# Alibi sliding attention with a token mixer: half loads for batch 0, units of 64 keys in the last two batches, the mask on VectorE, and an order that counts TensorE's instructions

## The chip, the core and the metric

The kernel runs on one core of a Trainium2 chip. The core has a matrix engine (TensorE, PE in the profile; its weight loads are listed apart as PEld), VectorE (DVE), ScalarE (ACT), GpSimd (POOL), SyncE (SP), and sixteen DMA engines that move data between the chip's memory and the core's. Matmul results land in PSUM, from which only ACT and DVE copy here. The metric is the time of one execution in microseconds on the device. Lower is better.

## The reference

Eight batches, eight heads, 576 positions, 64 values per head. Attention looks back over a window of 128 positions and adds a slope per head times the distance:

```python
slopes = 2.0 ** (-8.0 * (np.arange(H) + 1) / H)
bias = slopes[:, None, None] * (-np.abs(rel))[None, :, :]
mask = (rel >= 0) & (rel < window)                    # window = 128
scores = np.where(mask, scale * q @ k^T + bias, -1e9)
attn = softmax(scores)
x = attn @ v                                          # all heads side by side: 576 x 512
```

Then a mixer over the tokens, with 64 hidden columns:

```python
W_tok = 1/8 * (x @ w_q) @ (x @ w_k)^T                 # 576 x 576
out = np.maximum(W_tok @ x, 0.0) @ w_out              # 576 x 512, fp32
```

The kernel never forms W_tok: it computes G = (x w_k)^T x, which is 64 x 512, and then G^T (x w_q)^T.

## The kernel before

**Work of one batch.** The 576 positions are four blocks of 128 and a tail of 64; tails of two neighbouring batches share tiles. The names below are those of the planner's operations.

- Loads (L): q, k and v come as fp32 and are stored as fp16 by POOL's transfers (`dma_nat`, `dma_v`, `dma_tail`, `dma_vtail`, lines 504 to 523), one per block, rows of 64 values. Four batches' worth of q, k and v tiles exist (`NNAT`, `NV`). Batch 0's first two blocks of q and k are the exception: SP loads them as fp32 (`lf`, line 549) and a cast (C) makes them fp16.
- TQ and TT turn q and k by transposes on PE (64 rows a piece, line 347); ETQ and ETT copy the result from PSUM to `qkT`, on ACT or DVE.
- A unit (`add_unit`, line 654) is one key block of 128 and one half of the heads: QK (score matmuls against 256 query columns), EXP (ACT, 128 x 1024, into a `pt` tile), MUL (DVE, times `bias`, which holds exp of slope times distance and zeros outside the window). There are eight units in a batch and ten `pt` tiles.
- PV (`add_pv`, line 694) multiplies `pt` with v, which carries a column of ones for the row sums; X divides by the sums (DVE, lines 729 and 730).
- XT/EXT turn x; WQ, WK, G and MX are the mixer's matmuls with their copies EWQ, EWK, EG; RM is the relu (ACT or DVE); OUT (512-column matmuls with `wout`) and EO give the output tile; DO stores it.

**Constants.** POOL makes an identity (`make_identity`), an iota, and two `affine_select` passes that set positions outside the window to 1e9 (`mk_mask`, line 427); DVE copies the iota to fp32 in between; ACT makes `bias` with eight exponentials (`mk_bias`, line 469).

**What sets the order.** A list scheduler (`Order.solve`, line 234) places all operations: each has allowed engines with an occupancy and a latency, dependencies, PSUM banks, and a due time (`WANT`, a table of several hundred numbers). It takes the engine that can start first, and among what can start within `WINDOW` the lowest due time. Its result is the order in which instructions are emitted; every engine then runs its own list strictly in that order, and waits on semaphores. Until the planned time 45 us, idle PE gaps are filled with matmuls on zeros (`fill`). Stores of batches 1 to 5 (`LATE`) are issued by POOL after all its loads (line 962); the others go by SP.

## Time and profile before

| | |
|---|---|
| median of 3 runs | 140.56 us (140.37 to 140.99) |
| the profiled execution's own time | 141.34 us |
| its span (first to last instruction) | 139.5 us |
| mean granted TensorE clock | 0.997 |
| PE / DVE / ACT / POOL busy | 129.3 / 112.6 / 115.2 / 110.0 us |
| instruction queue | 18 packets, 0.29 MB |
| POOL's q, k and v loads, median from issue to landing | 5.9 to 6.1 us |

The profile is of one execution. Its page gives busy time by engine, the span cut in 40 slices with the busy share in tenths, the DMA queues, the chain of waits that ended last, and groups of instructions with count and mean duration. The trace behind it answers further: busy time in chosen windows, the instructions of one engine in order of time, who waited for whom. "busy" for PE is pipelined: a matmul's own duration includes its way through the array, so neighbours overlap, and start-to-start distances tell the cost of one in a row.

### The profile page before, as it was taken

What the parts mean: (1) busy time and instruction counts of PE and PEld (TensorE: products, weight loads), DVE (VectorE), ACT (ScalarE), POOL (GpSimd) and SP (SyncE); (2) the same over time, 40 slices, a digit from 0 to 9 for tenths busy, and PEclk for the clock granted to TensorE, in tenths of its full rate; (3) what the DMA queues carried; (4) which work ended last, traced back from release to release, by engine and by line L of the source; (5) the groups of instructions that cost most, each with busy time, mean ns of one, the idle gap of its engine ahead of it and who ended that gap; (6) DMA issues with size and microseconds to landing.
All of it is one profiled execution on the core that took longest, in us unless ns stands there. A gap on an engine that the chain in (4) does not pass through costs nothing.

```text
span 139.5 us, 5462 instructions
## 1 busy us (share of the span) xinstructions
PE 129.3 (93%) x2344; PEld 81.2 (58%) x2344; DVE 112.6 (81%) x250; ACT 115.2 (83%) x175; POOL 110.0 (79%) x145
## 2 busy tenths in 40 slices
PE   6999859998999999988999999999999999999980
PEld 2345447554676367766757567765666666865530
DVE  6648997659987899989999998899999989984400
ACT  6176988399669999999999989999999999676660
POOL 7899988899995899999999999999977745600000
PEclk9999999999999999999999999999999999999998
DMA  4999999999999999999999999999999993730494
GB/s 98 184 180 154 158 153 168 152 146 154 188 215 206 158 159 153 156 155 155 154 156 153 157 156 155 159 153 156 156 215 413 358 327 144 260 153 5 167 320 189
DMA packets 117127, 25.12 MB, mean 180 GB/s; under 512 B 113072, under 2 KB 114096, under 8 KB 117104
## 3 DMA queue, kind: packets, MB, share of 16 engines
q0 software_dynamic: 110912, 20.32, 169.0%
q1 hardware_dynamic: 6192, 4.46, 10.8%
q8 instruction: 18, 0.29, 0.8%
q14 instruction: 5, 0.04, 0.1%
HBM read 29.62 MB, written 9.44 MB: 280 GB/s over the span
## 4 chain that ended last, share of the span: by engine, by line
PE 60%; DVE 16%; POOL 8%; ACT 6%; DMA 5%; issue 2%; ACTq 0%; POOLq 0%; DVEq 0%
PE pair L344 52%; PE pair L347 8%; DVE pt L687 6%; DMA nat<-in_q_dram 5%; POOL nat L506 4%; ACT pt L680 4%; DVE x L730 3%; POOL vt L521 1%; POOL natt L513 1%; DVE inv L729 1%; DVE xtl L730 1%; DVE wqT L353 1%; DVE qkT L359 1%; DVE rm L843 1%; ACT xT L357 1%
## 5 line engine op out<-in xcount | busy, mean ns | idle before, releaser
L680 ACT ACTIVATE pt<-pair 128x1024 f16<-128x1024 f32 x64 | 62.2, 1034 | 2.3 <-PE pair L344 1.7
L687 DVE TENSOR_TENSOR pt<-pt,bias 128x1024 f16<-128x1024 f16 x48 | 32.0, 684 | 2.5 <-ACT pt L680 2.3
L344 PE MATMUL pair<-wout_sb,rm 128*128 128x512 f16 (+1 forms) x132 | 31.7, 373 | 0.2
L521 POOL DMA_DIRECT2D vt<-in_v_dram x32 | 30.1, 995 | 1.6 <-DMA natt<-in_q_dram 0.8
L506 POOL DMA_DIRECT2D nat<-in_k_dram x30 | 29.1, 997 | 0.5 <-DMA nat<-in_k_dram 0.3
L506 POOL DMA_DIRECT2D nat<-in_q_dram x30 | 29.0, 987 | 0.4 <-DMA natt<-in_k_dram 0.4
L344 PEld LDWEIGHTS <-pt 128*128 128x128 f16 x576 | 20.5, 97 | 6.2 <-issue 2.6
L344 PE MATMUL pair<-vt,pt 128*128 128x65 f16 x512 | 22.9, 193 | 0.4 <-ACT pt L680 0.4
L730 DVE TENSOR_TENSOR x<-pair,inv 128x512 f16<-128x512 f32 x32 | 22.1, 692 | 1.1
L344 PE MATMUL pair<-qkT 64*128 64x256 f16 (+2 forms) x320 | 22.1, 250 | 0.6 <-ACT pt L680 0.3
L351 ACT COPY osb<-pair 128x512 f32<-128x512 f32 x29 | 17.0, 596 | 5.7 <-PE pair L344 5.5
L344 PEld LDWEIGHTS <-rm 128*128 128x128 f16 x132 | 11.3, 97 | 11.8 <-issue 1.7
L357 ACT COPY qkT<-pair 128x1024 f32<-128x1024 f32 (+1 forms) x12 | 11.4, 949 | 7.7 <-PE pair L347 7.7
L344 PE MATMUL pair<-fill 128*128 128x512 f16 x52 | 15.4, 430 | 1.8 <-DVE fill L487 1.2
L918 POOL DMA_DIRECT2D out_dram<-osb x20 | 11.2, 574 | 6.6 <-ACT osb L351 3.6
L344 PEld LDWEIGHTS <-qkT 64*128 64x128 f16 x320 | 11.1, 94 | 8.0 <-issue 5.2
L347 PE MATMUL pair<-identh,nat 64*128 64x64 f16 x512 | 10.7, 190 | 1.3 <-DMA nat<-in_q_dram 0.9
L347 PEld LDWEIGHTS <-nat 64*128 64x128 f16 x512 | 9.2, 95 | 4.0 <-DMA nat<-in_q_dram 1.3
L687 DVE TENSOR_TENSOR pt<-pt,biasl 128x1024 f16<-128x1024 f16 x16 | 10.8, 683 | 0.0
L344 PE MATMUL pair<-xT,wqq_sb 128*128 128x320 f16 (+1 forms) x64 | 10.5, 286 | 0.3 <-DVE xT L359 0.3
L357 ACT COPY xT<-pair 128x512 f32<-128x512 f32 (+1 forms) x14 | 7.4, 527 | 3.6 <-PE pair L347 2.9
L359 DVE COPY qkT<-pair 128x512 f16<-128x512 f16 (+2 forms) x14 | 9.3, 686 | 1.3 <-PE pair L347 1.1
(63 smaller groups left out, 165.5 us busy)
## 6 DMA issues: line engine op xcount, KB each, us to landing
out_dram<-osb POOLq DMA_DIRECT2D x20, 256.0 KB, 4.6
vt<-in_v_dram POOLq DMA_DIRECT2D x32, 128.0 KB, 5.9
nat<-in_k_dram POOLq DMA_DIRECT2D x30, 128.0 KB, 6.0
nat<-in_q_dram POOLq DMA_DIRECT2D x30, 128.0 KB, 6.1
out_dram<-osb SPq DMA_DIRECT2D x11, 256.0 KB, 2.3
out_dram<-osb POOLq DMA_DIRECT2D x6, 128.0 KB, 4.2
natf<-in_q_dram SPq DMA_DIRECT2D x2, 256.0 KB, 4.7
natf<-in_k_dram SPq DMA_DIRECT2D x2, 256.0 KB, 5.4
```

What stands on the lines that cost most here:

```text
L344: hold(nc.tensor.matmul(*a, **k))
L347: hold(nc.tensor.transpose(*a))
L351: hold(nc.scalar.copy(out_ap, in_ap))
L353: hold(nc.vector.tensor_copy(out=out_ap, in_=in_ap))
L357: hold(nc.scalar.copy(out_ap.bitcast(FP32), in_ap.bitcast(FP32)))
L359: hold(nc.vector.tensor_copy(out=out_ap, in_=in_ap))
L506: return lambda: nc.gpsimd.dma_start(out=nat_s[b % NNAT][j][n], in_=src[b, :, P * n:P * n + P, :].transpose([1, 0, 2]))
L521: return lambda: nc.gpsimd.dma_start(out=vt_s[b % NV][t][:, :, 0:D], in_=v[b, :, P * t:P * t + P, :].transpose([1, 0, 2]))
L680: nc.scalar.activation(out=pt[:, 0:1024], in_=two(s.bank).rearrange("p e c -> p (e c)"), func=AF.Exp, scale=SCALE)
L687: ENG2[o.eng].tensor_tensor(out=pt[:, 0:1024], in0=pt[:, 0:1024], in1=bt, op=ALU.mult)
L730: nc.vector.tensor_tensor(out=x[r].rearrange("p (g h d) -> p g h d", g=2, h=4), in0=pxv[r, :, :, 0:64], in1=inv[r].unsqueeze(3).broadcast_ ...
L918: q.dma_start(out=out[b, P * st:P * st + P, c], in_=osb)
```

## The change

Four things are changed.

1. **Batch 0's first blocks by 4 heads.** `lf` loads one half of the heads at a time on SP: eight transfers of 128 x 256 values instead of four of 128 x 512, the first halves of both blocks ahead of the second halves. Each half has its own cast, its own turn (`add_tqh`) and its own copy to `qkT`, so that a unit of one half of the heads waits for that half only.
2. **The mask on VectorE.** POOL makes only the iota. DVE makes the identity from it (`is_equal`) and the distances with the window's bounds (`mk_wdist`, `mk_dist`), one set for 128-key units and one for 64-key units.
3. **Units of 64 keys in batches 6 and 7** (`NARROW = (3,)`, the pair number). A unit is then 64 keys and all eight heads: keys sit in partitions 0 to 63 for four heads and 64 to 127 for the other four, against 192 query columns. EXP and MUL take 768 columns instead of 1024. PV takes 64 keys at a time, two row halves in turn. v has a layout of its own for it, with two halves of the partitions for two groups of heads and all nine 64-key blocks, which four transfers of 64 partitions fill; the ones columns of those tiles are set again before, and the gaps in ten `pt` tiles are cleared. The other batches keep their units, renamed `add_wunit` and `wpv`; `pt` is now a flat list of ten tiles.
4. **The planner counts TensorE's instructions.** Every PE operation says how many instructions it has (`count`); `solve` adds a delay when 256 of them would be used up in less than `FETCH` us. `STRIDE` goes from 15.2 to 13.2 and the table of due times is a new one, so the order on all engines is new.

```diff
-NPT = 5
+NPT = 10
+W = 192
+NARROW = (3,)
-STRIDE = 15.2
+STRIDE = 13.2
+FETCH = 4.8
+CHUNK = 256
+AHEAD = 191
 WANT = {
...
+            if eng == "PE" and op.count:
+                gap, wait = at - free["PE"], 0.0
...
+                while sent > mark:
+                    came = max(at, came + (FETCH if came < 104.0 else FETCH - 1.0) if mark > AHEAD else 0.0)
+                    mark += CHUNK
+                    wait = max(wait, came - at)
+                if sent + op.count > mark:
+                    then = at + wait + occ * (mark - sent) / op.count
+                    least = came + (FETCH if came < 104.0 else FETCH - 1.0) if mark > AHEAD else 0.0
+                    wait += max(0.0, least - then)
+                    came = max(then, least)
+                    mark += CHUNK
+                sent += op.count
+                end, occ = end + wait, occ + wait
...
-    def mk_ident(o):
-        make_identity(nc, ident32)
-    def mk_mask(o):
-        nc.gpsimd.affine_select(out=wm, in_=wm, compare_op=ALU.is_ge, fill=1.0e9, base=0,
-                                pattern=[[1, 256]], channel_multiplier=-1)
-        nc.gpsimd.affine_select(out=wm, in_=wm, compare_op=ALU.is_ge, fill=1.0e9, base=127,
-                                pattern=[[-1, 256]], channel_multiplier=1)
+    def mk_idh(o):
+        nc.vector.tensor_scalar(out=identh, in0=wint[:, 0:P], scalar1=0.0, scalar2=1.0,
+                                op0=ALU.is_equal, op1=ALU.mult)
+    def mk_dist(o):
+        for x in range(2):
+            r = slice(64 * x, 64 * x + 64)
+            nc.vector.tensor_copy(out=wm[r], in_=wint[r, 64 * x:64 * x + W])
+        nc.vector.tensor_scalar(out=wlo, in0=wm, scalar1=-1.0e9, scalar2=0.0, op0=ALU.mult, op1=ALU.add)
+        nc.vector.tensor_scalar(out=whi, in0=wm, scalar1=-127.5, scalar2=1.0e9, op0=ALU.add, op1=ALU.mult)
+        nc.vector.tensor_tensor(out=wm, in0=wm, in1=wlo, op=ALU.max)
+        nc.vector.tensor_tensor(out=wm, in0=wm, in1=whi, op=ALU.max)
+        nc.vector.tensor_scalar(out=wm[64:128], in0=wm[64:128], scalar1=1.0 / 16.0, scalar2=0.0,
+                                op0=ALU.mult, op1=ALU.add)
+    def mk_wdist(o):
+        nc.vector.tensor_copy(out=wwm, in_=wint)
+        for s, a in ((-1.0e9, 0.0), (1.0e9, -127.5e9)):
+            nc.vector.tensor_scalar(out=wtmp, in0=wint, scalar1=s, scalar2=a, op0=ALU.mult, op1=ALU.add)
+            nc.vector.tensor_tensor(out=wwm, in0=wwm, in1=wtmp, op=ALU.max)
...
+    def dma_v(b, t, x):
+        return lambda: nc.gpsimd.dma_start(
+            out=vn(b % NV, t)[64 * x:64 * x + 64, :, :, 0:D],
+            in_=v[b, NHP * x + 2 * t:NHP * x + 2 * t + 2, :, :].rearrange("h (n t) d -> t (h n) d", t=64))
...
+        if key not in ones or ...:
+            ones[key] = add("ones", b, "", -200 + 20 * b, DVE(0.25 if narrow else 0.5), oldv, mk_ones(b % NV, narrow))
...
-        def lf(j, n):
+        def lf(j, n, u):
+            natf = spool.tile([P, DM], FP32, name="natf", tag="late", bufs=HELD)[:, 0:256]
+            hs = slice(NHP * u, NHP * u + NHP)
+            src = (q, k)[j][0, hs, P * n:P * n + P, :].transpose([1, 0, 2])
...
+    def add_tqh(n, u, want):
+        def em(o):
+            for j in range(2):
+                for c in range(2):
+                    for h in range(2):
+                        src = nat_s[0][j][n][64 * h:64 * h + 64, 4 * u + 2 * c:4 * u + 2 * c + 2, :]
+                        flip(halves(o.bank, 4, 1)[:, h, 2 * j + c, 0, :], src.rearrange("p a b -> p (a b)"), h)
...
     def add_unit(b, g, u):
+        s = 2 * g + u
+        pt = pt_s[(8 * b + s) % NPT]
+        ptd = pt[:, 64:PTW].rearrange("p (e a c) -> p e a c", e=2, a=2)[:, :, :, 0:W]
         def em(o):
             ps = two(o.bank)
+            for a in range(2):
+                for sk, c0, n in ((s, 0, W),) if s < 7 else ((7, 0, P), (8, P, 64)):
+                    for x in range(2):
+                        for e in range(2):
+                            r = slice(64 * e, 64 * e + 64)
+                            mm(ps[64 * x:64 * x + 64, e, W * a + c0:W * a + c0 + n],
+                               t[r, 1, 2 * x + a, 64 * sk:64 * sk + 64],
+                               t[r, 0, 2 * x + a, 64 * sk:64 * sk + n], start=True, stop=True)
...
+            def rz(o):
+                nc.vector.memset(pt[:, 0:1024].rearrange("p (n c) -> p n c", c=256)[:, :, 0:64], 0.0)
...
+    def npv(b, qt):
+        sv = [sk for sk in range(2 * qt - 2, 2 * qt + 2) if 0 <= sk < 9]
+        def em(o):
+            px = two(o.bank)
+            for a in range(2):
+                for e in range(2):
+                    for i, sk in enumerate(sv):
+                        c = 64 + 256 * (2 * e + a) + 64 * (2 * qt - sk)
...
+                        for x in range(2):
+                            r = slice(64 * x, 64 * x + 64)
+                            h = 2 * a + e
+                            mm(px[:, x, 65 * h:65 * h + 65], pt_s[(8 * b + min(sk, 7)) % NPT][r, c:c + P],
+                               vn(b % NV, a)[r, e, sk, 0:65],
+                               start=(i == 0), stop=(i == len(sv) - 1))
...
-        for ns in ([0], [1], [2], [3]) if b == 0 else ([0, 1], [2, 3]):
+        if b == 0:
+            for u in range(2):
+                for n in range(2):
+                    add_tqh(n, u, base(b, 0) - 4 + n)
+        for ns in ([2], [3]) if b == 0 else ([0, 1], [2, 3]):
...
-                add_unit(b, g, u)
+                (add_unit if b // 2 in NARROW else add_wunit)(b, g, u)
```

As the program is built, PE's list has 5,094 entries instead of 4,690, DVE's 270 instead of 251, ACT's 172 instead of 169, POOL's 137 instead of 145 and SP's 24 instead of 20 (rows that differ only in being repeated are counted as one on the engines other than PE).

More of the change, by code (lines that the diff above doesn't have):

```diff
@@ L492 @@
-    zeros = add("zeros", "", "", 0, DVE(0.55), [], mk_zeros)
-    zerop = add("zerop", "", "", -59, DVE(0.45), [], mk_zerop)
-    mask = add("mask", "", "", -298, {"POOL": (0.86, 0.86)}, [dist], mk_mask)
-    mkb = [add("bias", u, "", -240 + 10 * u, ACT(1.35), [mask], mk_bias(u)) for u in range(2)]
-    sets = [add("ones", i, "", -200 + 20 * i, DVE(0.5), [], mk_ones(i)) for i in range(NV)]
-    pads = add("pads", "", "", -297, ACT(1.3), [], mk_pads)
-    mkbl = [add("biasl", u, "", 6, DVE(0.55), [mkb[u]], mk_biasl(u)) for u in range(2)]
+    idh = add("idh", "", "", -290, DVE(0.29), [iota], mk_idh)
@@ new lines @@
+    zerop = [add("zerop", i, "", -59, DVE(0.55 if 0 in NARROW else 0.3), [], mk_zerop(i)) for i in range(2)]
+    if NARROW:
+        dist = add("dist", "", "", -300, DVE(1.6), [iota], mk_dist)
+        mkb = add("bias", "", "", -240, ACT(1.14), [dist], mk_bias)
+    wide = len(NARROW) < NB // 2
+    first = {}
+    for b in range(NB):
+        first.setdefault((b % NV, b // 2 in NARROW), b)
+    ones = {}
+    pads = add("pads", "", "", -297, ACT(1.3), [], mk_pads)
+    if NARROW:
+        mkbl = add("biasl", "", "", 6, DVE(0.4), [mkb], mk_biasl)
@@ L501 @@
+    if wide:
+        zeros = add("zeros", "", "", 0, DVE(0.55), [], mk_zeros)
+        wdist = add("wdist", "", "", -90, DVE(1.5), [iota], mk_wdist)
+        wmkb = [add("wbias", u, "", -70 + 10 * u, ACT(1.35), [wdist], mk_wbias(u)) for u in range(2)]
+        wmkbl = [add("wbiasl", u, "", 6, DVE(0.55), [wmkb[u]], mk_wbiasl(u)) for u in range(2)]
     nat, natt, vt = {}, {}, {}
@@ L536 @@
     late, issues = [], []
-    loads = {}
+    loads, one_b = {}, {}
     def add_loads(b):
@@ L695, in ptc, with wpv @@
+    def wpv(b, qt):
         def ptc(kb, h, cur):
```

250 lines of the change are left out of this document (160 added, 90 removed), and 289 rows, old and new, of the table WANT.

## The prediction

> **What bounds the kernel now.** I read the page first, then the windows by stage, the chain of waits, and the timelines of single engines. The page's busy line and three of its 40-slice rows (3.49 us a slice):
>
> ```profile
> PE 129.3 (93%) x2344; PEld 81.2 (58%) x2344; DVE 112.6 (81%) x250; ACT 115.2 (83%) x175; POOL 110.0 (79%) x145
> ...
> DVE  6648997659987899989999998899999989984400
> ACT  6176988399669999999999989999999999676660
> POOL 7899988899995899999999999999977745600000
> ```
>
> No engine is the bound throughout. ACT and DVE have holes before about 42 us, are full until about 118 us, and empty again. POOL, which only issues transfers, is full until 105. The windows (columns: length, then busy time of PE, PEld, DVE, ACT, POOL with instruction counts):
>
> ```profile
> 20.00:28.00 8.00, 8.00 (x190) 5.33 (x187) 5.79 (x13) 4.49 (x6) 6.67 (x10) 1.00 1.75 158
> ...
> 60.00:85.00 25.00, 23.91 (x512) 16.06 (x509) 23.43 (x45) 24.10 (x37) 25.00 (x31) 1.00 2.42 155
> ...
> 106.00:118.00 12.00, 11.66 (x240) 7.44 (x239) 11.49 (x21) 11.79 (x20) 7.29 (x14) 1.00 0.80 301
> 118.00:124.00 6.00, 6.00 (x141) 4.78 (x141) 5.59 (x13) 3.67 (x7) 3.02 (x6) 1.00 0.74 265
> ```
>
> In the middle DVE, ACT and POOL are all above 93%; from 118 on only PE is full. The chain of waits:
>
> ```profile
> 12.94 6.91 DMA nat<-in_q_dram
> 19.84 0.05 issue
> 19.89 0.64 PE pair L347 x32
> ...
> 124.73 10.94 PE pair L344 x88
> ```
>
> It starts on batch 1's q and k, which land at 19.84, and ends on PE's output matmuls. Three timelines fix the stages: ACT's exponentials, POOL's last loads, PE's turn of batch 7's first blocks.
>
> ```profile
> 12.44 7.44 ACT L680 ACTIVATE pt<-pair 128x1024 f16<-128x1024 f32 x8 [0.78 <-PE pair L344]
> ...
> 117.52 1.96 ACT L680 ACTIVATE pt<-pair 128x1024 f16<-128x1024 f32 x2
> ```
>
> ```profile
> 98.95 1.09 POOL L506 DMA_DIRECT2D nat<-in_q_dram  x1
> 99.81 1.10 POOL L521 DMA_DIRECT2D vt<-in_v_dram  x1
> ```
>
> ```profile
> 106.01 0.64 PE L347 MATMUL pair<-identh,nat 64*128 64x64 f16 x32
> ```
>
> A load lands 6.0 us after its issue (page, transfers), so batch 7's last q or k lands at 98.95 + 5.95 = 104.9 and is turned 1.1 us later. The loads run only just ahead of the work.
>
> So there are four stages: start (to 20), a middle where ACT, DVE and loads are nearly equal, ACT's finish (106 to 119.5, the last exponential), PE's finish.
>
> **The change, part by part.**
>
> *q and k by 4 heads.* Four SP transfers of 256 KB become eight of 128 KB, first halves of both blocks first. Now the four casts start at 4.5, 4.9, 8.2 and 10.3 us (DVE timeline), and the first exponential at 12.44. In the new order of ACT's instructions the first exponential stands behind the cast that needs the seventh of the eight halves; between the third quarter (8.2) and the fourth (10.2) that is about 9.2, and with cast and queue 10.0. Ends: 8.2 (six halves suffice) and 12.4 (nothing). I take 10.0: ACT starts 2.4 us earlier, and its eight exponentials (7.44) end at 17.5 instead of 19.9. The cost is four more SP issues (0.44 to 0.9 us, SP waits for nothing then) and four more small casts, about 0.3 us each; ACT takes some of them, before its first exponential.
>
> *What is late next.* Batch 1's first turn needs the 12th POOL load before and the 15th after, since batch 0's last v blocks go ahead of it. The 15th issue of before is at 15.54 and lands 6.5 later, at 22.0. So ACT, done at 17.5, waits; batch 1 begins up to 2.2 us later, batch 0's v work and the small weights (loads 16 and 17, before 20 and 21) earlier. Between 20 and 28 ACT is busy 4.49 of 8 us, so there is a hole into which batch 0's second half can move.
>
> *Mask on DVE.* POOL loses the identity (0.49 us) and two mask instructions (0.80) with the gaps around them (about 0.7): its issues run up to 2 us earlier from the fifth on. DVE gains eleven instructions like the 128x256 cast (0.27): 3 us, and ACT four exponentials for the second bias (0.25 each, scaled from 0.31). DVE is idle for 2.3 us before 8.23; without that cover the first multiplication, now at 13.50, would wait up to 3 us, still before batch 1's load.
> Does an earlier issue land earlier? The row says little: POOL has a gap of 0.52 before its mask at 6.03, yet loads go on landing 0.85 apart, behind a queue of 6 us. From 25.5 to 40 us issues and landings both come 0.87 apart. I take 0.3 us earlier for the whole stream; ends 0 and 1.8.
> [...]
>
> *Units of 64 keys, batches 6 and 7.* An exponential falls from 1024 to 768 columns: with 1.03 us for 1024 and 0.40 for 256 that is 0.82, back to back 0.71 instead of 0.92: 16 x 0.21 = 3.4 us off ACT, half in each batch. A multiplication falls from 0.68 to about 0.54 (ends 0.51 in proportion, 0.95 if four short rows ran at the rate of the fp32 copies, 0.69 for 512): 16 x 0.14 = 2.2 off DVE. DVE gets ten clears at about 0.15 (rows: 0.085 for 32 words, 0.27 for 256) and four of 0.07: 1.8 back. PE: per batch 72 score matmuls instead of 40 and 136 PV matmuls instead of 72. Two 64-row operations run side by side in the trace: 32 turns take 0.64 us and 16 PV matmuls of 128 rows 0.66; less the last one's own 0.19 that is 15 ns and 31 ns each. At 16 the PV costs 2.2 us instead of 2.1 a batch; at 30, 4.1. Score matmuls of 192 columns go by fours, estimate 22 ns (end 40, by pairs): 1.6 against 1.9. I take the side-by-side prices: PE even. POOL issues 109 loads instead of 110, but the eight v loads of batches 6 and 7 carry 18 rows a partition instead of 16, which evens that out.
>
> *The wait that it adds.* Batch 7's v tiles are cleared anew on DVE once all of batch 3's PV is read, and the v load behind that clear is POOL's 78th, now issued at 72.1; everything behind it in POOL's queue, 31 loads, waits too. Batch 3's last PV now ends at 71.7 and its eviction would put the clear near 72.7. With the work 2 us ahead it is at 71. So POOL may stand still for up to 1 us. Loads that meet no queue land 4.7 us after issue (27 to 38 us) against 6.0 here, so 1.3 us is covered; if the work were not ahead, it would cost the stream up to 0.7. I take 0.
>
> *The order.* The count is used only in planning. It moves batch 7's second turn ahead of its first, and the first now needs the last load but one (q, block 1).
>
> **The sum,** in the span of the profiled execution (139.5; its time is 141.34, so 1.84 lies around it; median of the runs 140.56).
> - Last turn of batch 7: the load but one lands at 98.95 + 5.95 - 0.3 = 104.6; the turn's eviction on ACT starts at about 105.4 instead of 106.7: -1.3. The 2.4 us lead of the start and the lighter exponentials of batch 6 (-1.7) would bring ACT there by about 104, so the load decides, and PE, in order, waits with it.
> - From there to batch 7's last score unit ACT has eight exponentials (5.7), three relus, two output copies, two xT, one wkn and the eviction (0.92): 10.4 us; before it was 12.5 by the same prices and took 12.8. PE's own work on that stretch is 11 us (turns 0.5, outputs 4.4, scores 1.6, PV6 1.8, the rest 2.7), so PE is late next: the last unit comes at 116.2 instead of 118.0, -0.5 beyond the 1.3.
> - From the last unit to the last output PE had 16.6 us of work in 17.7; after, 16.3: -0.3, and I add 0.2 for denser code. The tail of 3.85 (copy, store, end) stays.
> Together -1.9: span 137.6, and 140.56 - 1.9 = 138.66, say 138.6 us.
>
> **Rivals.**
> *Delivery of TensorE's instructions decides: slower.* 4,688 instructions came in 18 packets of the instruction queue, 260 each. The densest long windows are 190 + 187 in 8 us and 141 + 141 in 6: 47 a us. In the new order 588 instructions stand between batch 7's second turn and batch 6's last PV, about 8.5 us of work (69 a us), and 256 around PV7 in 3.3 us. Were 47 the most, the first would take 12.5 (+4.0), the second 5.4 (+2.1). Together +6.1 against the gain of 1.9; below about 59 a us the change is slower by over 0.7: +0.7 to +4.2, 141.3 to 144.8. For it: packets share queues that are 9 tenths busy. Against it: PE's list of waits names an engine or a load for each wait, and short bursts run far faster (32 turns and their loads in 0.64).
> [...]
> *The stream follows POOL: more gain.* If landings follow the issues by 1.8, the last turn comes at 103.1 and ACT decides at 104: a further -1.2 to -1.8, 136.6 to 137.2. For it: issue-paced landings from 25.5 to 40. Against it: the 6 us queue.
> *The start's lead is spent.* Batch 1's first turn 2.2 us later eats the 2.4, the work arrives at batch 7 as now and POOL's new wait bites: -0.5 to +0.7, 140 to 141.2. Against it: the hole between 20 and 28.
> *The narrow forms don't run side by side.* PV at 30 and scores at 40 ns add 3.3 us of PE a batch, all of batch 7's in the PE-bound end: +1.4, 142.
>
> **How the numbers follow.** Half a per cent, 0.7 us, is about what can be told from no change. Forecast (137.6 to 139.8): 0.46. More gain (136 to 137.6): 0.17. Lead spent: 0.14. Delivery: 0.14. Narrow forms: 0.09. Faster 0.46 + 0.17 + 0.02 of the spent lead = 0.65; same 0.13; slower 0.22. Low end 136.2 (the rival's best with a little of both ends), high end 141.9: that leaves out most of the delivery case and half of the narrow one. The likeliest case's own range is 137.6 to 139.8.
>
> **What would show it.** First exponential near 10.0; batch 1's first turn near 22; exponentials of 768 columns near 0.82, multiplications near 0.54; PV of batches 6 and 7 at about 16 ns a matmul; batch 7's last turn near 105 right behind its load; last exponential near 117. PE gaps in batches 6 and 7 with no releaser would speak for delivery, and a last turn well before 104.5 against the load stream as the limit.

## The result, and the profile after

The changed kernel takes 144.25 us (median of 4 executions, 143.80 to 144.98) against 140.61 for the kernel before: 1.026 times as long, 95% interval 1.021 to 1.031. The forecast was 138.6 in a range of 136.2 to 141.9. The profiled execution took 143.80, its span is 141.8, where the prediction's sum gave 137.6. Ratios leave out executions that took over 1.5% longer than the fastest of the same kernel.

First the page's busy line and the three 40-slice rows (3.55 us a slice):

```profile
PE 131.8 (93%) x2546; PEld 80.1 (56%) x2546; DVE 115.7 (82%) x280; ACT 115.6 (82%) x182; POOL 107.5 (76%) x140
...
DVE  6995897789976899899979998999999898792400
ACT  7496691799849995799899999999799978957761
POOL 6997789999999788999919999998950978610000
```

ACT's busy time has not fallen, although sixteen exponentials are shorter: casts, bias and evictions that went over to ACT took it back. POOL now has a hole at 71 to 74 us. The windows, with the columns as before:

```profile
20.00:28.00 8.00, 7.64 (x161) 5.18 (x160) 6.59 (x15) 3.84 (x7) 8.00 (x11) 1.00 2.18 161
60.00:85.00 25.00, 24.47 (x480) 15.37 (x475) 23.44 (x50) 23.99 (x34) 21.96 (x26) 1.00 2.22 143
106.00:118.00 12.00, 11.99 (x353) 7.67 (x352) 11.45 (x25) 10.89 (x19) 6.92 (x13) 1.00 0.71 260
118.00:124.00 6.00, 6.00 (x133) 3.70 (x129) 4.74 (x12) 5.71 (x11) 4.44 (x10) 1.00 0.97 333
```

The chain of waits still begins with a load of batch 1. It now goes on over POOL's issues and a v load to the turn of batch 1's first blocks at 25.27, and it ends on the output matmuls:

```profile
9.67 7.79 DMA nat<-in_k_dram
18.09 3.49 POOL nat L585 x4
21.59 3.67 DMA vt<-in_v_dram
...
133.41 4.63 PE pair L389 x24
```

The middle looks as it did. What moved most is in the first 28 us. ACT's timeline (start, length, what; in brackets the idle time before it and what ended that):

```profile
11.99 0.37 ACT L402 COPY qkT<-pair 128x256 f32<-128x256 f32 x1 [1.25 <-PE pair L392]
12.26 0.41 ACT L396 CAST nat<-natf 128x256 f16<-128x256 f32 x1
12.57 1.96 ACT L794 ACTIVATE pt<-pair 128x1024 f16<-128x1024 f32 x2
15.58 1.94 ACT L794 ACTIVATE pt<-pair 128x1024 f16<-128x1024 f32 x2 [1.05 <-PE pair L389]
17.76 3.77 ACT L794 ACTIVATE pt<-pair 128x1024 f16<-128x1024 f32 x4 [0.24 <-PE pair L389]
24.64 0.75 ACT L402 COPY xT<-pair 128x512 f32<-128x512 f32 x2 [3.11 <-PE pair L392]
...
27.78 1.02 ACT L794 ACTIVATE pt<-pair 128x1024 f16<-128x1024 f32 x1
```

Batch 0's exponentials start at 12.57 (12.44 before, 10.0 in the prediction), have holes, and end at 21.5 (19.9 before, 17.5 predicted). Batch 1's first one comes at 27.78, before at 22.46. Its turn at 25.27 is listed as waiting for a v load, but the q and k that it turns had landed by 21.74. Two more timelines say why the first is late, DVE's (first five lines) and PE's (last three):

```profile
8.37 0.74 DVE L505 COPY wbiasl<-wbias 128x384 f32<-128x384 f32 x2
9.06 0.25 DVE L532 MEMSET pt<- 128x32 uint32 x5
9.23 0.58 DVE L398 CAST nat<-natf 128x256 f16<-128x256 f32 x1
9.74 0.89 DVE L556 COPY biasl<-bias 128x256 f32<-128x256 f32 x2
10.07 0.70 DVE L398 CAST nat<-natf 128x256 f16<-128x256 f32 x1
```

```profile
7.23 2.55 PE L389 MATMUL pair<-fill 128*128 128x512 f16 x11
9.71 0.39 PE L389 MATMUL pair<-qkT 64*128 64x256 f16 x4
...
25.27 0.65 PE L392 MATMUL pair<-identh,nat 64*128 64x64 f16 x32 [0.21 <-DMA vt<-in_v_dram]
```

The casts at 9.23 and 10.07 take halves that landed at 8.01 and 8.45; copies of the bias tiles and clears stand ahead of them in DVE's list. On PE eleven dummy matmuls on the constant tile `fill`, which only keep TensorE busy, run from 7.23 to 9.78, ahead of the first scores, whose operand was ready at 8.50. The kernel fixes their number from the gaps in its solved order; where a landing is later than planned, they still stand ahead of the work that waited for it.

**A way to follow a static order.** Solving its order, the kernel gives every step a planned start, and each engine keeps that order on the chip. The step's start in the trace (of one profiled execution) less that planned start is its lag. In us, trace / plan = lag:

| step | before | after |
|---|---|---|
| first exponential, batch 0 | 12.44 / 11.51 = 0.93 | 12.57 / 9.80 = 2.77 |
| first exponential, batch 1 | 22.46 / 20.67 = 1.79 | 27.78 / 22.77 = 5.01 |
| first turn, batch 3 | 53.05 / 50.75 = 2.30 | 56.21 / 51.40 = 4.81 |
| turn of blocks 0 and 1, batch 7 | 106.01 / 104.06 = 1.95 | 109.50 / 103.60 = 5.90 |
| last full output | 134.63 / 132.10 = 2.53 | 137.00 / 130.78 = 6.22 |

At the last output the new order is planned 1.32 earlier and lags 3.69 more; the sum, +2.37, is the difference of the two profiled spans (2.3). The medians differ by 3.6: the profiled execution of before took 0.7 us more than its median, that of after 0.45 less, so some 1.2 us of the loss lie outside of this table. Of the 3.69, 3.22 are there at batch 1's first exponential, which is also planned 2.10 later than in the old order. Over the next 110 us the lag grows by 1.21, before by 0.74.

### The profile page after: what moved, and what is told of

Same layout as the page of the kernel before. It is cut to its first block, busy times and chain, and to the rows that moved or that the text cites. A ratio compares the mean times of both kernels' runs of the same rounds, so it can differ in the third digit from the quotient of the medians.

```text
span 141.8 us, 5900 instructions
## 1 busy us (share of the span) xinstructions
PE 131.8 (93%) x2546; PEld 80.1 (56%) x2546; DVE 115.7 (82%) x280; ACT 115.6 (82%) x182; POOL 107.5 (76%) x140
## 4 chain that ended last, share of the span: by engine, by line
PE 62%; DVE 9%; POOL 8%; DMA 8%; ACT 8%; issue 2%; POOLq 0%; DVEq 0%
PE pair L389 52%; PE pair L392 10%; ACT pt L794 7%; DMA nat<-in_k_dram 5%; POOL nat L585 5%; DMA vt<-in_v_dram 3%; DVE pt L801 2%; POOL vt L601 2%; DVE x L914 1%; POOL natt L592 1%; DVE rm L1029 1%; DVE xT L404 1%; ACT qkT L402 1%; DVE rmt L1029 1%; DVE inv L913 1%
## 5 line engine op out<-in xcount | busy, mean ns | idle before, releaser
L794 ACT ACTIVATE pt<-pair 128x1024 f16<-128x1024 f32 x48 | 47.0, 1035 | 2.4 <-PE pair L389 2.0
L801 DVE TENSOR_TENSOR pt<-pt,wbias 128x1024 f16<-128x1024 f16 x36 | 24.0, 684 | 1.5 <-ACT pt L794 1.4
L396 ACT COPY osb<-pair 128x512 f32<-128x512 f32 (+1 forms) x30 | 17.1, 575 | 9.5 <-PE pair L389 9.3
L389 PEld LDWEIGHTS <-pt 128*128 128x128 f16 (+1 forms) x704 | 20.2, 96 | 6.0 <-issue 3.2
L389 PE MATMUL pair<-vt,pt 128*128 128x65 f16 (+1 forms) x656 | 23.2, 192 | 0.4
L389 PE MATMUL pair<-qkT 64*128 64x256 f16 (+4 forms) x384 | 22.1, 247 | 0.5 <-DVE rm L1029 0.3
L389 PE MATMUL pair<-fill 128*128 128x512 f16 x62 | 18.4, 414 | 2.1 <-DVE fill L558 1.2
L389 PEld LDWEIGHTS <-qkT 64*128 64x128 f16 (+1 forms) x384 | 11.0, 99 | 9.1 <-issue 5.7
L835 ACT ACTIVATE pt<-pair 128x768 f16<-128x768 f32 x16 | 12.8, 826 | 0.7 <-PE pair L389 0.5
L392 PE MATMUL pair<-identh,nat 64*128 64x64 f16 x512 | 11.2, 191 | 1.3 <-ACT nat L396 0.8
L389 PE MATMUL pair<-xT,wqq_sb 128*128 128x256 f16 (+1 forms) x64 | 10.4, 287 | 0.0
L1029 DVE TENSOR_SCALAR rm<-pair 128x512 f16<-128x512 f32 x15 | 9.8, 682 | 0.0
```

Of the source, the lines that this page charges most:

```text
L389: hold(nc.tensor.matmul(*a, **k))
L392: hold(nc.tensor.transpose(*a))
L396: hold(nc.scalar.copy(out_ap, in_ap))
L794: nc.scalar.activation(out=pt[:, 0:1024], in_=two(s.bank).rearrange("p e c -> p (e c)"), func=AF.Exp, scale=SCALE)
L801: ENG2[o.eng].tensor_tensor(out=pt[:, 0:1024], in0=pt[:, 0:1024], in1=bt, op=ALU.mult)
L835: nc.scalar.activation(out=ptd, in_=two(q.bank)[:, :, 0:2 * W].rearrange("p e (a c) -> p e a c", a=2), func=AF.Exp, scale=SCALE)
```

## The experiments

The unit for comparison is the ratio to the kernel before on the same chip, with its 95% interval; "+x us" is that ratio less 1, times 140.6. The changed kernel is +3.7.

**1. The start taken apart.** Two theories: what the start loses is carried to the end (S), or the full middle swallows it (M).

e1_mask_later reorders three groups of steps after the order is solved; e2_fewer_fills cuts dummies; e3_both does both; e4_whole loads whole blocks.

```diff
+    plan = later(plan, ['dist', 'bias', 'biasl'], 'ETQ1.2')
+    plan = later(plan, ['wbias0'], 'ETQ0.1.0')
+    plan = later(plan, ['wbiasl0', 'wbiasl1', 'zerop1'], 'Ck0.1.1')
...
+FILLS = {'QK0.0.0': 5, 'TQ0.2': 0, 'TQ0.0.1': 0, 'QK0.1.0': 2, 'TQ0.1.1': 0, 'TQ0.3': 0, 'QK0.1.1': 0, 'QK0.2.0': 0}
+        n = min(n, FILLS.get(f"{op.kind}{op.batch}.{op.part}", n))
...
-                nc.sync.dma_start(out=natf.rearrange("p (h d) -> p h d", h=NHP), in_=src)
+                if u == 0:
+                    nc.sync.dma_start(out=natf_s[j, n].rearrange("p (h d) -> p h d", h=H), in_=src)
```

> Changed kernel with the mask's instructions taken out of the way of the first blocks' casts: the mask and bias of the 64-key units (needed from 95 us on) behind batch 1's second turn, the wide bias's first four exponentials on ACT behind the second eviction, the shifted wide biases and half of the clears behind the last cast; nothing else moves. Theory S (the start decides: what is lost there is carried one for one to the end, because from 25 us on every engine keeps a constant distance to the order and the loads land 2 to 5 us before they are used): the casts of the second head halves run within 0.6 us of their landing instead of 1.2 to 1.6 after it; PE still has its dummy matmuls ahead of the second half's first turn, so only the last half gains: first exponential at about 12.3 instead of 12.57, third at 15.0 instead of 15.6, end 0.3 to 0.9 us earlier (143.4 to 144.0). Theory M (the middle decides: ACT and DVE are full there, so a head start is spent): 144.25 +- 0.2.

> Changed kernel with 7 instead of 28 dummy matmuls between batch 0's second turn and its third block's scores (no result uses them); nothing else moves. Theory S: first scores at 8.6 to 8.9 instead of 9.71, second half's first turn at 10.8 (bound by its cast, 10.07 + 0.7) instead of 11.66, first exponential at about 11.7; end 0.4 to 1.0 us earlier (143.2 to 143.8). If a colder TensorE makes the first turns and scores slower, up to 0.5 of that is given back. Theory M: 144.25 +- 0.2.

> The two edits together. Theory S: the second half's first turn comes at about 9.3 to 9.8, the first exponential at 10.2 to 10.8, the last half (landing 11.8) gives the third exponential at about 14.2 to 14.6; end 1.2 to 2.2 us earlier (142.0 to 143.0), more than the two edits alone give in sum. Theory M: 144.25 +- 0.3.

> Changed kernel with batch 0's first blocks loaded as before by four transfers of 256 KB, cast and turned by halves in the same order. Landings as before (3.7, 4.6, 8.2, 10.2) instead of halves that land at 3.2 to 11.8. Theory S: first scores only after 10.9, first exponential at 12.4 to 13.0 as now, but the second half no longer waits for 11.8: third exponential at 14.3 to 15.0 instead of 15.6; end 0.3 to 1.0 us earlier (143.2 to 144.0). If the halves are worth what the prediction took (1.5 to 2.4 us): 1.5 us later or more. Theory M: 144.25 +- 0.3.

Measured: e1 1.070 (1.066 to 1.073), e2 1.019 (1.015 to 1.023), e3 1.060 (1.054 to 1.065), e4 1.065 (1.060 to 1.069). Three of the four missed by 5 us or more, because of side effects of the edits that teach something all the same.

What holds the first exponential can be read before those effects strike. It comes at 12.57 in the changed kernel, at 12.49 with the mask's steps moved behind the casts (e1), at 11.66 with fewer dummies (e2), and at 10.94 with both (e3, third exponential at 14.29). So the dummies hold it up first, and behind them the steps ahead of the casts in DVE's list.

In e1 the mask's instructions, moved to 30 us, stand in DVE's list from 30.6 to 34.9, ACT waits 3.48 us for them, and batch 1 stops. TensorE then stands still from 32 to 36 us, and its granted clock is 0.50 from 32.8 to 43.0; what that adds to the loss was not measured. The lag grew from 4.95 at 27.7 us to 12.35 at batch 3's first turn and is 14.05 at the last full output (144.83 against 137.00 in the changed kernel): the stop of the middle is never made good. e3 carries the same mistake in the middle. In e4 PE idled between 5 and 8.6 us, its clock fell (windows: length, busy times, then the granted clock as the third number from the end):

```profile
8.00:12.00 4.00, 2.61 (x13) 1.10 (x14) 1.41 (x10) 3.33 (x12) 4.00 (x5) 0.50 2.34 166
```

and the static dummies ran ahead of the first scores, now at 14.54, at a granted clock of 0.50 from 8 to 12 us and of 0.71 in the mean from 12 to 16. Its lag at batch 1's first exponential is 10.29, 5.28 more than the changed kernel's; its time is 5.4 us more. A delay of the start, then, reached the end whole here. M falls for delays.

In e2 the first scores came at 8.48 and the lag at 26 us was 3.45 instead of 5.01, although the granted clock fell to 0.50 from 11.6 to 18.4. At batch 5's first turn the lead over the changed kernel was 1.2 us; at 106 us most of it was lost within one group of matmuls, in this execution (144.19; the median gained 1.1 us on the changed kernel):

```profile
106.05 0.30 PE L390 MATMUL pair<-x,wkn 128*64 128x256 f16 x1
107.62 0.62 PE L390 MATMUL pair<-x,wkn 128*64 128x256 f16 x7 [1.27 <-issue]
```

"issue" means that nothing in the trace was waited for. The stop is at PE's instruction 3,772, at the edge of a block of 256 (the edges fall at about 191 + 256k: the changed kernel's 5,094 instructions have 20 of them, and its trace has 20 packets of the instruction queue).

**2. Is it the delivery of instructions?** e6_thin_fills keeps the number of dummies (so every later instruction keeps its place in its block) and makes 23 of them 64 columns wide (the expectation counts 21); e8_whole_thin does it for whole loads; e7_turns puts 1,024 extra turns in at two places; e5_wide67 is read below.

```diff
+        n, full = FILLS.get(f"{op.kind}{op.batch}.{op.part}", (n, n))
+        for i in range(n):
+            c = 512 if i < full else 64
+            mm(pairs[...][:, ..., 0:c], fill[:, 0:P], fill[:, 0:c], start=True, stop=True)
...
+        if (op.kind, op.batch, op.part) == ('TQ', 3, 0):
+            turns(nc, two(op.bank).bitcast(F16), fill, identh, 1024)
...
+    turns(nc, pairs[0].bitcast(F16), fill, identh, 1024)
```

> The run with fewer dummy matmuls lost its lead of 1.5 us at 106 us in a stop of 1.27 us inside one group of matmuls, at TensorE instruction 3,772, next to the edge of a block of 256. Here the 21 dummies are kept but have 64 columns instead of 512, so that every later instruction keeps its place in its block. Theory D (late delivery of a block, which depends on where the edges fall): the stop goes, the lead of 1.5 us at 25 us reaches the end: 142.4 to 143.0. Theory R (the stop is a matter of chance in one execution or comes from another cause): a stop of 1 us or more between 100 and 115 us again, 143.5 to 144.3.

> Changed kernel with 1,024 extra turns of a constant tile (2,048 TensorE instructions, eight blocks) put in twice: ahead of batch 3's first turn, while loads stream, and after the last output matmul, when nothing but the last stores moves; their results are used by nothing. Measures delivery by itself. At the rate of the turns in the trace (32 in 0.64 us) eight blocks take 20 us, 2.6 us a block. Theory D: under the load stream 4.3 to 5.6 us a block with stops at the edges (34 to 45 us for the turns), clearly less after the loads have ended. Prefetch theory (blocks stream far ahead): 20 us in both places, no stops.

> Changed kernel with batch 0's first blocks loaded by four whole transfers as before, cast and turned by halves, and the dummies placed for that: eleven moved ahead of batch 0's second turn, the others 64 columns wide, their number unchanged. Theory S: last quarter lands at 10.2 instead of 11.8 to 12.1; first scores at 11.0, first exponential at 11.6 to 12.2, the eight of batch 0 close together until 19.3 to 19.8 (21.5 in the changed kernel); lag to the order at 25 us 3.0 to 3.5 instead of 5.0; end 1.5 to 2.1 us earlier, 142.1 to 142.8. If the halves are worth something: no better than the run with thin dummies alone by 0.5 or more.

e7 measures the delivery, in one execution. PE's timeline in the first group of extra turns:

```profile
56.82 2.53 PE L321 MATMUL pair<-identh,fill 64*128 64x64 f16 x162
62.63 3.15 PE L321 MATMUL pair<-identh,fill 64*128 64x64 f16 x128 [3.29 <-issue]
67.45 3.60 PE L321 MATMUL pair<-identh,fill 64*128 64x64 f16 x128 [1.67 <-issue]
72.55 3.60 PE L321 MATMUL pair<-identh,fill 64*128 64x64 f16 x128 [1.50 <-issue]
77.38 2.04 PE L321 MATMUL pair<-identh,fill 64*128 64x64 f16 x128 [1.23 <-issue]
80.83 1.35 PE L321 MATMUL pair<-identh,fill 64*128 64x64 f16 x81 [1.41 <-issue]
```

PE stops after every 128 matmuls, which with their weight loads are one block. (Its granted clock was 0.54 from 62.6 to 77.4; that stretches the turns, 3.60 us for 128 against 2.04 at 1.00, not the spacing, as each block ends in a stop.) While loads stream (until 77) a block comes every 4.8 to 5.1 us, 50 to 53 instructions a us; afterwards, and in the group at the end of the kernel, every 3.5 to 4.0. A packet of the instruction queue starts 2.5 to 2.8 us after an edge under load (3.1 after the first), 1.1 without, takes about 1 us, and PE goes on 1.3 to 1.5 us after its end. So one block was on its way at a time here: an edge had to be crossed before the next was fetched. PE stops because a block of turns takes less time (2.04 us at a clock of 1.00) than the block behind it takes to come (3.5 us and more).

e6: 1.014 (1.010 to 1.017), +1.9. Batch 0's exponentials now run without a hole from 11.72 to 19.16. The stop at 106 is gone as theory D said, but another of 1.12 us stands at 124.8, again at an edge (4,796 of 4,799): the fetch before it began 3.5 us after its edge instead of the 2.0 there in the changed kernel. D's late delivery fits both stops; that the place of the edges alone decides where it strikes does not: the time from edge to fetch varies. The changed kernel itself shows no stop above 0.42 us at an edge, so in this execution delivery is not what made it slow.

e8: 1.043 (1.039 to 1.046). PE was busy for 1.39 of 4 us from 8 to 12, and its granted clock was 0.50 from 11.6 to 21.9:

```profile
8.00:12.00 4.00, 1.39 (x14) 0.60 (x14) 0.66 (x4) 2.71 (x9) 3.55 (x5) 0.95 2.34 162
12.00:16.00 4.00, 3.73 (x55) 2.08 (x55) 3.19 (x15) 3.83 (x12) 3.71 (x5) 0.50 2.42 156
16.00:20.00 4.00, 4.00 (x57) 1.96 (x57) 3.78 (x8) 3.21 (x4) 3.08 (x5) 0.50 2.29 154
```

TensorE was idle for 2.6 of the 4 us from 8 to 12, mostly before the clock fell at 11.6. Less came before it elsewhere: the granted clock in these traces changes in steps of 3.41 us, and it fell after a step with 1.55 us of idle in e2 (8.18 to 11.59) and in e4 (4.07 to 7.48). No run measures the least idle time ahead of a fall. The run does not answer what the halves are worth. It gives one more point on the start: batch 1's first exponential at 29.93, +6.0.

**3. All dummies thin, the mask, the halves, and a control.** e9 widens the list of e6; e10 leaves the mask out; e11 also issues the second halves from ACT; e12 is the kernel before with thin dummies from 10.5 us of its order on.

```diff
     def mk_dist(o):
+        nc.vector.memset(wm, 0.0)
     def mk_wdist(o):
+        nc.vector.memset(wwm, 0.0)
...
-                nc.sync.dma_start(out=natf.rearrange("p (h d) -> p h d", h=NHP), in_=src)
+                (nc.scalar if u else nc.sync).dma_start(out=natf.rearrange("p (h d) -> p h d", h=NHP), in_=src)
...
+        c = 512 if op.start < THIN else 64
```

> As the run with thin dummies (e6_thin_fills), and the other dummies up to 45 us are 64 columns wide too, among them the thirteen around batch 0's v work, where the lag to the order grew from 1.85 to 3.0 us. Theory S (what the start loses reaches the end): lag at 25 us 1.9 to 2.2 instead of 3.0, end 0.8 to 1.1 us earlier than that run, so 141.5 to 142.2, with single executions up to 1.5 later where a block of instructions comes late. Theory M: 142.8 as that run. If TensorE's clock falls with the thinner dummies: 0.5 or more later.

> As e9_thin_all, with the eleven VectorE instructions of the mask replaced by two clears: the attention's mask and bias are left out of the result. Prices the mask on VectorE by itself. Theory K (the mask holds up the casts and with them the whole start): casts of the second halves at their landing (8.3 and 8.8 instead of 9.2 and 10.2), first exponential at 10.4 to 10.8 instead of 11.7, end 0.8 to 1.3 us earlier than e9_thin_all. Theory H (the last half's landing at 11.7 to 12.1 holds the third exponential at 13.5 whatever comes before it): first exponential earlier, third not, end within 0.4 of e9_thin_all.

> As e10_no_mask (mask and bias left out), and the four second halves of the first blocks are issued by ACT ahead of its other work instead of by SP behind the first four. Theory H: they are all issued by about 3 us instead of 5.6, the last lands at 9.5 to 10.5 instead of 11.8, third exponential at 12.0 to 12.6 instead of 13.5, end 0.9 to 1.5 us earlier than e10_no_mask. If the 16 DMA engines, not the issue, set the landing: last half at 11 or later, end within 0.4 of e10_no_mask.

> The kernel before, with its dummies from 10.5 us of its order on 64 columns wide instead of 512 (number unchanged), among them seven that stand ahead of batch 1's second turn from 25.02 to 26.64, whose load landed at 25.17. Control for the dummies: if they cost the old order time as they cost the new one, batch 1's second turn comes 1.0 to 1.5 us earlier and the end 0.5 to 1.4 us earlier, 139.2 to 140.1; if the dummies only matter where the landings come later than planned, 140.56 +- 0.3.

e9: 1.010 (1.006 to 1.013), +1.3, so the dummies alone cost the changed kernel 2.3 of its 3.7 us. ACT in e9:

```profile
11.66 7.43 ACT L797 ACTIVATE pt<-pair 128x1024 f16<-128x1024 f32 x8
...
24.68 1.02 ACT L797 ACTIVATE pt<-pair 128x1024 f16<-128x1024 f32 x1
```

The lag at batch 1's first exponential is 1.91 instead of 5.01, at the last output 5.57 instead of 6.22: a start 3.1 us earlier is worth 2.3 by the ratios and 0.65 in this execution, whose lag grows from 1.64 at batch 3's first turn to 5.57. Where that went: loads of q and k, used 1.9 to 5.4 us after landing in the changed kernel, now arrive just in time (batch 3's first turn 53.04, load 52.97; batch 6's second turn 98.15, load 98.03), and a late block stops PE for 0.84 us at 124.7. Batch 1's first turn comes at 21.91, 0.27 us behind its last load (21.64), against 19.89 before: now the load decides there.

e10: 1.005 (1.001 to 1.009), 0.6 us less than e9 with overlapping intervals; first exponential at 11.61, third at 13.49, as in e9 (11.66, 13.48). The mask's own instructions are not what holds the start there, so K falls. H doesn't hold either, as it had the first exponential earlier: DVE waits 3.56 us (4.7 to 8.25) for ACT's bias exponentials, because the copies of their results still stand ahead of the casts, and the casts of the second halves stay at 9.21 and 10.02.

e11: 1.015 (1.010 to 1.019). The four second halves land at 3.7 to 8.6 instead of 8.2 to 11.9, so the order of issue set the landing here. But ACT, which issues them, makes its first cast at 5.32 instead of 3.05 (e6), PE idles (0.98 us ahead of 5.77, 1.03 ahead of 8.47), the granted clock is 0.57 from 8 to 12, and the start is lost again.

e12: 0.995 (0.991 to 0.999). Batch 1's second turn came at 25.57 instead of 26.64, as expected, and the old order gains 0.7 us (0.1 to 1.2) from thin dummies, against 2.3 in the new one. The medians of all executions, 140.68 and 140.84, are only 0.2 apart, so the gain is small at best. It is the fastest kernel of the study that computes all of the result.

Put together, batch 1's first exponential (in one execution of each) against the end (by the ratios):

| run | first exponential, batch 1 | end, against before |
|---|---|---|
| e9 | 24.68 | +1.3 |
| e10 (no mask) | 24.98 | +0.7 |
| e6 | 25.76 | +1.9 |
| e2 | 26.22 | +2.6 |
| e11 (no mask) | 26.58 | +2.0 |
| after | 27.78 | +3.7 |
| e8 | 29.93 | +6.0 |
| e4 | 33.06 | +9.1 |

From 27.78 up, a us at the start is a us at the end (5.4 for 5.28); below, down to e9, about three quarters of one (2.3 for 3.10). Without the mask the end is some 0.8 us earlier than this line.

**4. The narrow units.** e5 swaps batches 6 and 7 back to wide units in the changed kernel's own order, e17_thin_wide67 does so in e9 (emission only; the list of steps stays).

```diff
+        em, wex, ml = wunit(b, g, u)
...
-            nc.scalar.activation(out=ptd, in_=two(q.bank)[:, :, 0:2 * W].rearrange("p e (a c) -> p e a c", a=2),
-                                 func=AF.Exp, scale=SCALE)
+            wex(q.bank)
...
+        em = wpv(b, qt)[2]
```

> Changed kernel in its own order, but batches 6 and 7 computed with the wide units of before (v by blocks of 128 keys and one more tail load, no new clears). Theory N (the narrow units are worth what the prediction took: 0.21 us of ACT a unit, 0.14 of DVE, TensorE even): the sixteen exponentials bring back 3.4 us on ACT, and the end comes 1.0 to 2.5 us later than 144.25 (145.2 to 146.8). Theory O (the order sets the pace and ACT has holes there): 144.25 +- 0.5. Theory W (the narrow forms cost TensorE more than they save): 0.5 to 1.5 us earlier.

> As e9_thin_all (142.28, with a stop of 1.03 us for a late block of instructions at 124.7), but batches 6 and 7 with the wide units of before, some 290 TensorE instructions fewer in the last 40 us. In the changed kernel the same swap cost 1.1 us. Theory N (the narrow units are worth 1.1 us wherever the start stands): 143.0 to 143.8. Theory D (with the work 2 to 3 us earlier their 290 instructions meet late blocks, and the swap takes the stops away): 141.9 to 142.6, no stop over 0.5 us after 100 us.

e5: 1.033 (1.030 to 1.036), 1.0 us more than the changed kernel; theory N, at its lower end. e17: 1.015 (1.009 to 1.021), 0.8 more than e9 with overlapping intervals, between the two theories; it has no stop after 100 us. The narrow units help by about 1 us in the changed kernel, not by the 3.4 that they take off ACT.

**5. Which engine bounds the middle?** Open was why a repaired start and lighter units do not end ahead of the kernel before. Theory P: TensorE's own work; A: ACT and DVE. In batches 2 to 4, e13 leaves out a quarter of the columns of each exponential and multiplication, e14 half of those of each output matmul; e15 and e16 do the same to the kernel before.

```diff
+            n = 768 if b in (2, 3, 4) else 1024
+            nc.scalar.activation(out=pt[:, 0:n], in_=...[:, 0:n], func=AF.Exp, scale=SCALE)
...
+                w = n // 2 if b in (2, 3, 4) else n
+                mm(one(o.bank)[:, 0:w], lt, wout_sb[:, db, c.start:c.start + w], start=(db == 0), stop=(db == 3))
```

> Changed kernel with the 24 exponentials and 24 multiplications of batches 2 to 4 over 768 of their 1,024 columns (a quarter of those attention weights is left out): 5.0 us less on ACT, 3.5 us less on DVE, TensorE and loads as they are. Theory P (from about 35 us on TensorE's own work sets the pace: it is idle for 0.7 us of the changed kernel between 60 and 140): end within 0.6 of 144.25. Theory A (ACT and DVE, full from 40 to 118, set the pace, as the prediction read the page): 2 to 4 us earlier.

> Changed kernel with the output matmuls of batches 2 to 4 over half of their columns (13 outputs, half of each left out of the result): 52 x 0.108 = 5.6 us less on TensorE, the same number of instructions, ACT, DVE and loads as they are. Theory P: 2.5 to 5 us earlier (139.2 to 141.8), less than 5.6 because loads, 2 to 5 us ahead, and denser instructions come next. Theory A: within 0.8 of 144.25.

> The kernel before with the same cut of the exponentials and multiplications of batches 2 to 4. Theory P: within 0.6 of 140.6. Theory A: 2 to 4 us earlier.

> The kernel before with the same cut of the output matmuls of batches 2 to 4. Theory P: 1 to 3 us earlier (its loads come only 1.0 to 4 us ahead of their turns). Theory A: within 0.8 of 140.6.

e13: 1.017 (1.011 to 1.023), 1.3 us less than the changed kernel for 5.0 us of ACT and 3.5 of DVE. e14: 1.022 (1.017 to 1.026), 0.7 less for 5.6 us of TensorE. On the kernel before: e15 0.998 (0.995 to 1.001), e16 0.994 (0.991 to 0.997). Taken alone, e14 fits A and e15 fits P; e13 and e16 fit neither, so neither theory holds over the four. (The intervals of e13 and e14 overlap that of the changed kernel.) The window 60 to 110 of e14, and then of the changed kernel:

```profile
60.00:110.00 50.00, 45.83 (x1072) 32.62 (x1072) 47.17 (x107) 47.53 (x69) 42.18 (x51) 1.00 2.38 151
```

```profile
60.00:110.00 50.00, 49.46 (x1067) 31.76 (x1063) 47.05 (x106) 47.68 (x69) 41.06 (x49) 1.00 2.23 151
```

TensorE's cut appears as idle time of TensorE; ACT and DVE go on as they were, at 94 to 95%. All three are within 6% of full and hand work to each other in a fixed order, so relief of one was worth between a twentieth and a quarter of itself; that the fixed order is the reason is argued, not shown.

**6. The halves once more.** e18_whole_warm has whole loads and more full dummies.

```diff
+FILLS = {'QK0.0.0': (0, 0), 'TQ0.2': (3, 2), 'TQ0.0.1': (1, 1), 'QK0.1.0': (3, 2), ..., 'TQ0.1.0': (19, 19)}
```

> As e9_thin_all, but the first blocks come by four whole transfers as before and nineteen dummies of full width stand ahead of batch 0's second turn, some full ones behind it, so that TensorE's clock does not fall as in e8_whole_thin (granted 0.5 to 0.6 there from 10.6 to 21 us); the number of dummies is unchanged. If loading by halves is worth what the prediction took, 1.5 to 2.4 us: batch 0's last exponential at 20.5 or later (19.1 in e9_thin_all) and the end 1.0 us or more later, 143.3 or more. If the halves bring nothing, because their last piece lands 1.7 us later than the last whole one (11.8 to 12.0 against 10.2): last exponential at 19.2 to 20.0, end within 0.6 of 142.28.

1.020 (1.013 to 1.027), 1.5 us more than e9, near the 1.0 of the first theory, but single executions ran from 143.39 to 147.53. In the profiled one (146.28) the clock was not kept up, as the comparison needs: TensorE was idle for 2.6 us of the step before 7.7 us and ran at 0.50 to 11.2, and the last quarter landed at 11.81. Inconclusive: what halves are worth against whole loads stays open.

One part needs no run. With FETCH set to 0 the kernel solves to the same list, step for step: the counting of instructions changes nothing for these due times. The part of the change that is an order is its new due times alone, and it is they that put batch 7's second turn ahead of its first.

## Why the prediction was wrong

- **The start was mis-sized: this step failed first.** "I take 10.0", then "its eight exponentials (7.44) end at 17.5". Measured 12.57 and 21.5. Those 4.0 us are nearly the miss in the span (4.2), but by medians the miss is 5.6. The sum priced a landing and a cast. The seventh half landed at 9.95 (9.2 forecast), which is only 0.75 of the 2.57. The rest is the list: eleven dummies ran until 9.78 ahead of scores whose operand was ready at 8.50, and casts stood behind bias copies (9.23 and 10.07 for halves landed at 8.01 and 8.45), so the second half's turn came at 11.66, its copy at 11.99 and the exponential at 12.57. With fewer dummies and the mask's steps behind the casts it came at 10.94 (e3). The dummies were not in the sum at all; e9 shows 2.3 us for them at the end. The holes behind it come from the last half, also without a price, which landed at 11.80. Without the dummies' width batch 0 still ends 1.6 us later than forecast (19.1 in e9).
- **"The load decides" for batch 7's last turn: wrong.** Its load landed at 106.63 (predicted 104.6), the turn came at 109.50. Loads had 1.9 to 5.4 us to spare; the list, 5.9 us behind its plan, decided. The eviction came at 110.22 (105.4 forecast), and the last scores ended 4.6 us late (120.8 for 116.2). For the same reason batch 1's load, forecast for 22.0, landed at 21.74 and was used at 25.27; there the forecast of the load was right and the step that waited for it was not. I took the stream of before, where loads are late, for the limit of a kernel in which the work had become later.
- **POOL's new wait: sized at up to 1 us, 3.04 measured**, behind batch 3's last PV:

```profile
70.11 1.03 POOL L601 DMA_DIRECT2D vt<-in_v_dram  x1
74.17 0.86 POOL L596 DMA_DIRECT2D vt<-in_v_dram  x1 [3.04 <-PE pair L389]
```

  With q and k loads 1.9 to 5.4 us ahead of their use, no cost of it is seen here.
- **The mask: nearly right in effect.** The twelve instructions take 4.2 us, not 3; leaving them out gains about 0.6, not clear of the noise (e10). Not priced was that bias copies would stand ahead of the casts: with fewer dummies, moving the mask's steps away brings the first exponential from 11.66 to 10.94 (e2, e3). What that is worth at the end was not measured, as e3 lost it in the middle.
- **The narrow prices: right.** Exponential 0.826 (0.82), multiplication 0.553 (0.54), clear 0.165 (0.15), PV 17.8 ns a matmul (16): two batches of PV take 4.85 us against 4.90. Scores 29 ns (22), 4.2 us for two batches against 5.2. Their worth, about 1 us, was smaller than the sum made it, since ACT's share hardly counts.
- **From the last scores to the end: nearly right.** 137.6 - 116.2 = 21.4 predicted; 141.8 - 120.8 = 21.0. The working has only PE full there; DVE was busy for 5.59 of the 6 us from 118 to 124.
- **The rivals.** "The start's lead is spent" had the place, but its price stopped at 141.2: it reckoned with a lead of 0 and not with a start slower than before. "More gain" was added up wrongly: 138.6 less 1.2 to 1.8 is 136.8 to 137.4, not 136.6 to 137.2. "Delivery" had the slower sign and a rate (47 a us) near what e7 measured under load (50 to 53), but the changed kernel's own trace has no such stop; stops of about 1 us appear in runs with an earlier start (e2, e6, e9).
- **What stays open:** why e9, whose batch 0 ends 0.8 us ahead of the kernel before and which has the narrow units, still ends 1.3 behind. Three things are seen: its batch 1 starts 2.2 us later (24.68 against 22.46), with the turn right behind a load that now comes after batch 0's v; late blocks stop PE for 1.1 us in two stops; loads come on time to 0.1 us. None was taken away by itself, and how much belongs to the new due times was not separated. "The start's lead is spent" named this later batch 1.

## What to carry to other kernels

In a kernel whose engines follow a list fixed in advance, read the lag of each step against its planned start before any engine's busy share: if it is constant, what was lost where it began is what the end shows. Here that held for delays; of an earlier start three quarters reached the end. Price filler work like any other instruction, because a static filler added to late arrivals here (2.3 us) instead of covering them. Don't book an engine's relief at its full time where the others are as full: here 5 us off one were worth 0.3 to 1.3.

## What the runs showed of the hardware

- TensorE got its instructions by blocks of 256, the next one fetched only once an edge was crossed: 4.8 to 5.1 us a block beside a load stream, 3.5 to 4.0 without (e7). Dense turns, 2.04 us for the 128 of a block at a clock of 1.00, stopped for 1.2 to 3.3 us at each edge.
- The granted clock changed in steps of 3.41 us. It was 0.50 after a step with 2.3 us of idle (e8) or 2.6 (e18), and also after 1.55 (e2, e4) and 1.3 (e12, 16.4 to 19.8). With thin dummies between the same steps it stayed at 1.00 at the start in e6, where PE was busy for 3.30 of 4 us from 8 on and 3.32 from 12 on, and in e9.
- A transfer of 128 KB issued at 4.60 behind four of POOL's landed after 7.2 us in the changed kernel; the same halves issued from two engines by 2.4 us all landed by 8.6 (e11).
